# New instruction lists for the last two head pairs of an LSH attention, and a last eviction dealt between ACT and VectorE

## The chip, the cores and the metric

One core of one Trainium2 chip runs the whole program. The metric is the device time of one execution in microseconds, as the median of several runs; lower is better. The program before the change takes 677.83 us (three runs, 676.93 to 678.04).

## What is computed

The reference is an attention in which a query only sees the keys of its own hash bucket, followed by a top-1 mixture of experts (MoE) over the tokens that the attention gives. Inputs are fp32: q, k and v of 4 batches x 8 heads x 768 positions x 64, a projection to 6 hash bits, a gate, and 8 experts of 512 -> 1024 -> 512. Cut to what matters:

```python
q_bits = (einsum('bhsd,dk->bhsk', q, proj) > 0); k_bits = (einsum('bhsd,dk->bhsk', k, proj) > 0)
mask = bucket(q_bits)[..., :, None] == bucket(k_bits)[..., None, :]
scores = where(mask, q @ k.T / sqrt(64), -1e9)
attn = exp(scores - max) / (sum + 1e-9)          # per head, 768 x 768
x = (attn @ v)  ->  3072 tokens x 512
e = argmax(x @ w_gate);  gate = softmax(x @ w_gate)[e]
y = gate * (relu(x @ w1[e]) @ w2[e])
```

## The kernel before

**Work and stages.** The 32 heads are taken as 16 pairs, g = 0 to 15. Each pair has 12 score tiles (128 queries of one head against all 768 keys; two heads x six blocks of queries). The MoE follows: tokens are sorted by expert in DRAM (`sorted_rows`), each expert's rows are read back, and two matrix multiplications per expert follow. Every fp32 operand of the MoE is split into a high and a low part, and three products are summed.

**Step letters.** A pair is written as a list of short names that `step` (L1101 onwards) turns into instructions in that order; a "-" behind a name means the pair before. Pair 0 has the list HEAD, pairs 1 to 13 PLAN, pair 14 NEXT and pair 15 LAST. The scheduler keeps the order of the list on each engine, so a list sets five queues at once. The steps that the prediction speaks of:

- S: scores of one tile, four matmuls on PE (L307, L309) into the PSUM tile "s" (3 buffers). R: masked minimum on VectorE (DVE, L319), which frees that tile. X: exp on ACT (L325).
- T: four transpositions on PE (L339) into the PSUM tile "t" (2 buffers); E: their copy to SBUF, on ACT (L406, suffix a) or DVE (L404, suffix v). Some tiles are turned another way, by step D: a 32x32 block transposition on DVE (L376), and after the last of a pair 16 DMAs (L383) that SyncE (SP) issues, into `pt` (for pair 15 `pq`).
- V: probabilities times values on PE, 24 matmuls. In pairs up to 14, V0 and V2 (L415) are the two halves of the tiles that the 16 DMAs turned, eight DMAs for each half; V1 (L429) takes the tiles turned on PE. In pair 15, V0 takes the tiles of T and V1 the others (both L429). O is the copy of the result (ACT, L445), M the reciprocal of the sums (DVE), K the product with the gate's weights (PE, L470), L its copy to the token rows `xr` (DVE, L480).
- C: one scatter of 128 token rows to `sorted_rows`, an indirect DMA that GpSimd (POOL) issues (L599). Y0: two DMAs on SP that read the first expert's rows into `xd` (L810). x, g, h: these rows transposed on PE (L867) and split (ACT L869, DVE L871).
- W: load of expert weights by SP (`raw`, or `xhe`, a tile that serves as a load buffer first; L765). n and t: the high part of a quarter of a weight chunk (nP on POOL L1034, nA on ACT L1032) and its low part (tP on POOL, tV on DVE, both L1040), taken in turn from a list of 16 quarters.
- m: first matrix multiplication (L888), u and d its relu and low part (ACT L902, DVE L904); the second is L963.

**What holds a step.** Steps on one engine run strictly in order. A scatter (C) that comes behind Y0 in the list writes `sorted_rows`, which Y0's DMAs read, so it waits until both `xd` loads have landed.

**The tail.** The last tile of tokens (98 rows) is done in two halves of 256 columns by `youts` (L984): 24 matmuls each (L1000), a copy scaled by the gate value (first half DVE L1006, second ACT L1004), and an indirect DMA out (L1007). `FIRST` (L947) is the order in which the second matrix multiplication of the first rows sums its eight hidden blocks; each needs its u and d done.

Of the kernel before, what the change touches and what calls it, by code (L numbers as in the profile page):

```python
# [11 lines left out]
AF = mybir.ActivationFunctionType  # L12
OP = mybir.AluOpType
AX = mybir.AxisListType

B, H, S, D = 4, 8, 768, 64
# [5 lines left out]
DM = H * D  # L22
N = B * S
# [8 lines left out]
M0 = float(2 ** 34)  # L32
# [22 lines left out]
def lsh_attention_moe(ctx, tc, qk, qk2, v, proj, wg, w1, w1p, w2, w2p, out):  # L55
    nc = tc.nc
# [80 lines left out]
    C = {}  # L137
# [607 lines left out]
    P2 = {}  # L745
# [43 lines left out]
    XG, IX, XH, HH, YT, GT = {}, {}, {}, {}, {}, {}  # L789
# [107 lines left out]
    M1 = {}  # L897
# [46 lines left out]
            t = len(range(q, nb, 4))  # L944
            nc.sync.dma_start(YR[n][32 * q:32 * q + 32, :t, 128 * a:128 * a + 128], YB[n][32 * a:32 * a + 32, q::4][:, :t])

    FIRST = (6, 1, 5, 3, 2, 4, 0, 7)  # L947

    def yout(n, j, mid=None):
        r, o, c = PH[n]  # L950
# [3 lines left out]
        if n + 1 == len(PH) and j + 1 == len(tiles_of(c)):  # L954
            youts(n, j, i, pw)
            return
        if by_token(n):
            p = ps.tile([128, 512], F32, name="s", bufs=3)
            k = 0
            for f in range(8) if n else FIRST:  # L960
                w = CH[4 * r + 2 + f // 4]
# [24 lines left out]
    def youts(n, j, i, pw):  # L986

        r = PH[n][0]
        y = P2["p"].tile([128, DM], F32, name="y", bufs=2)
        ix = P2["p"].tile([128, 2], I32, name="ix2")  # L990
        for s in range(2):
            nc.vector.tensor_scalar(ix[:, s:s + 1], IX[n][:, j:j + 1], 2.0, float(s), op0=OP.mult, op1=OP.add)
        for s in range(2):
            cs = slice(s * DM // 2, (s + 1) * DM // 2)
            p = ps.tile([128, 512], F32, name="s", bufs=3)
            k = 0
            for f in range(8):
                w = CH[4 * r + 2 + f // 4]
                for a, b in ((0, 0), (1, 0), (0, 1)):
                    nc.tensor.matmul(p[:pw, :DM // 2], HH[n][b][:, f, i:i + pw], w[:, a, f % 4, cs],  # L1000
                                     start=(k == 0), stop=(k == 23))
                    k += 1
            if s:
                nc.scalar.activation(y[:pw, cs], p[:pw, :DM // 2], AF.Copy, scale=GT[n][:pw, j:j + 1])  # L1004
            else:
                nc.vector.tensor_scalar(y[:pw, cs], p[:pw, :DM // 2], GT[n][:pw, j:j + 1], None, op0=OP.mult)  # L1006
            st = nc.gpsimd.indirect_dma_start(out=out.rearrange("n (s d) -> (n s) d", s=2),  # L1007
                                              out_offset=bass.IndirectOffsetOnAxis(ap=ix[:pw, s:s + 1], axis=0),
                                              in_=y[:pw, cs], in_offset=None, bounds_check=2 * N - 1, oob_is_err=False)
            for q in outs:  # L1010
                tc.declare_no_dep(st.ins, q.ins, reason="other parts of the rows")
            outs.append(st)
# [10 lines left out]
    def weight_half(op, x):  # L1023
# [33 lines left out]
    """.split()  # L1057

    NEXT = """
        Z2 S1 S0 P5 R0 G Z2 S8 S3 M0- H R1 R3 T50- Z2 Z2 X0 T51- Q Q R8 S2 T52- S9 R2 E50a- E51a- E52v- Q X1 P1 R9 Z2  # L1060
        D0 A2 X2 V1- X3 S5 S4 S6 V0- V2- O1- R4 R5 I S7 X4 X8 Q X9 D1 X5 S10 T41 W0 W1 S11 P3 P4 T40 W2 P6 R6 B D2 O0-
        P0 X6 W3 R7 R10 T42 A1 K1- E41a E40v X10 K0- P2 U X7 E42v R11 C A0 N L1- P7 L0- C X11 C
    """.split()

    LAST = """
        nP S3 C nA T30- E30a- T50- tP S0 R3 T31- C T51- tP S1 W4 T32- S2 nP E50v- E31a- X3 T52- tP S4 E52a- E51v- S5 R1
        S9 nP R2 E32a- R0 R5 X2 V1- nP S7 X0 X1 D1 X5 Y0 R4 S8 X4 R9 S6 D0 T20 R6 tP O1- R8 V0- nP X9 nP X6 M0- R7 X8
        nA V2- T21 C tV E21v S11 T41 nP E20a O0- R11 tP T22 E41a S10 nP tP E22a T40 K1- tP X11 x2 x0 K0- R10 X10 L1- X7
        E40v g2 L0- tP W5 g0 M0 nP T50 h2 E50a V0 h0 T51 T42 O0 E42a nA K0 T30 E30a tP T31 E51v M1 T52 L0 m1 E31a tP
        E52v r0 r0 r0 u1 T32 m6 r0 E32v W6 V1 u6 m7 O1 r0 K1 nP tV m5 m3 W7 tP r0 u5 d6 d1 nP c0 tP nA u7 L1 r1 r1 r1  # L1070
        r1 m2 u3 m0 m4 tP d5 u2 d7 r1 r1 d3 u4 d2 c1 u0 nP d4 tP d0
    """.split()

    SCAT = {}
# [188 lines left out]
    for n in range(1, len(PH)):  # L1263
        c0 = 4 * (PH[n][0] + 1)
# [28 lines left out]
    with tc.If(C["n"] > 0):  # L1293
        with tc.For_i(0, C["n"], 1) as i:
# [16 lines left out]
            p = ps.tile([128, 512], F32, name="t", bufs=2)  # L1311
# [5 lines left out]
            for f in range(8):  # L1317
                p = ps.tile([128, 512], F32, name="t", bufs=2)
# [3 lines left out]
            p = ps.tile([128, 512], F32, name="s", bufs=3)  # L1322
            for f in range(8):
                nc.tensor.matmul(p, ht[:, f], wb[:, f], start=(f == 0), stop=(f == 7))
            y = sp.tile([128, DM], F32, name="oy")
# [32 lines left out]
```

## Time and profile before

| | |
|---|---|
| median of 3 runs | 677.83 us (676.93, 677.83, 678.04) |
| profiled execution, its own time | 676.77 us |
| its span, first to last instruction | 675.0 us |
| mean granted TensorE clock | 0.999 |
| PE busy | 665.9 us (99%) |
| DVE, ACT, POOL busy | 467.4, 409.7, 468.0 us |
| DMA | 138.51 MB, mean 205 GB/s |

The span leaves 1.8 us of the profiled time outside it. In the rows below, times are microseconds from the span's start; "busy" is time in which an engine computed, and what stands in brackets behind a row is how long the engine had been idle before it and which instruction or DMA ended that idle time.

### The profile page before, as it was taken

How to read it: one execution, taken by the hardware profiler on the slowest of the kernel's cores; microseconds unless marked ns; L12 is line 12 of the kernel's file. 1: busy time of each engine (PE TensorE's matmuls, PEld its weight loads, DVE VectorE, ACT ScalarE, POOL GpSimd, SP SyncE). 2: the span in 40 equal slices, each digit the busy share in tenths (PEclk: the TensorE clock that was granted, in tenths of full speed). 3: DMA queues.
4: the chain of work that ended last, by engine and by line, in shares of the span. 5: the costliest groups of instructions: out<-in, count | busy, mean ns of one | idle time of the engine just before them, and what ended most of it. 6: DMA issues, size and time to landing. Idle time of an engine off the chain costs nothing.

```text
span 675.0 us, 12607 instructions
## 1 busy us (share of the span) xinstructions
PE 665.9 (99%) x4359; PEld 564.6 (84%) x4359; DVE 467.4 (69%) x878; ACT 409.7 (61%) x817; POOL 468.0 (69%) x524
## 2 busy tenths in 40 slices
PE   8999999999999999999999999999999999999997
PEld 4777887788777787788777888899999999989896
DVE  8999889988899889898984545351443645363761
ACT  7977887788778887878775225443444444534410
POOL 7878666977797779777866646855476684959622
PEclk9999999999999999999999999999999999999999
DMA  7689999888889788987896258657548484867203
GB/s 282 209 247 285 260 267 274 217 243 245 230 241 272 188 236 240 265 236 195 239 291 173 101 192 237 162 180 171 156 160 217 131 214 152 220 204 221 102 12 44
DMA packets 74321, 138.51 MB, mean 205 GB/s; under 512 B 16609, under 2 KB 37345, under 8 KB 74256
## 3 DMA queue, kind: packets, MB, share of 16 engines
q1 hardware_dynamic: 66528, 118.57, 61.7%
q0 software_dynamic: 7584, 19.10, 9.7%
q8 instruction: 35, 0.57, 0.4%
q14 instruction: 30, 0.25, 0.2%
q10 hardware_dynamic: 144, 0.02, 0.0%
HBM read 63.39 MB, written 26.33 MB: 133 GB/s over the span
## 4 chain that ended last, share of the span: by engine, by line
PE 95%; ACT 2%; issue 1%; DVE 1%; POOL 0%; POOLq 0%
PE s L888 22%; PE t L415 12%; PE s L927 11%; PE s L307 10%; PE s L963 10%; PE s L309 10%; PE t L339 8%; PE t L429 7%; PE t L470 3%; PE t L264 2%; PE t L104 1%; ACT e L325 1%; ACT qk L215 1%; ACT pq L406 0%; POOL out_dram L1007 0%
## 5 line engine op out<-in xcount | busy, mean ns | idle before, releaser
L325 ACT ACTIVATE e<-e,m 128x768 f32<-128x768 f32 x192 | 178.2, 930 | 37.2 <-DVE e L319 35.6
L319 DVE TENSOR_SCALAR_CACHE_REDUCE e<-s 128x768 f32<-128x768 f32 x192 | 176.1, 951 | 26.2 <-PE s L309 20.3
L784 POOL TENSOR_TENSOR w<-raw,w 128x512 fp32r<-128x512 f32 x112 | 142.3, 1298 | 32.1 <-ACT w L783 31.0
L888 PE MATMUL s<-xh,w 128*128 128x456 f32 (+6 forms) x672 | 123.9, 345 | 0.0
L888 PEld LDWEIGHTS s<-xh,w 128*128 128x128 f32 x672 | 120.0, 188 | 3.1
L904 DVE SCALAR_TENSOR_TENSOR hh<-s,hh 128x256 fp32r<-128x256 f32 (+7 forms) x64 | 35.5, 555 | 89.6 <-ACT hh L902 89.5
L376 DVE STREAM_TRANSPOSE z<-e 128x1536 f32<-128x1536 f32 x52 | 90.7, 1763 | 2.3 <-issue 0.9
L415 PE MATMUL t<-pt,vt 128*64 128x256 f32 x720 | 81.0, 381 | 0.0
L902 ACT ACTIVATE hh<-s 128x256 fp32r<-128x256 f32 (+7 forms) x64 | 31.3, 489 | 75.2 <-PE s L888 75.2
L927 PE MATMUL s<-hh,w 128*128 128x456 f32 (+3 forms) x384 | 74.6, 355 | 0.0
L927 PEld LDWEIGHTS s<-hh,w 128*128 128x128 f32 x384 | 71.3, 188 | 2.7
L415 PEld LDWEIGHTS t<-pt,vt 128*64 128x64 f32 x720 | 50.4, 137 | 27.6 <-issue 3.2
L783 ACT ACTIVATE w<-raw 128x512 fp32r<-128x512 f32 x112 | 66.3, 622 | 9.0 <-DMA raw<-in_w1p_dram 8.7
L339 PE MATMUL t<-ident,e 128*128 128x128 f32 x468 | 68.7, 277 | 1.2 <-DVE pt L404 0.5
L339 PEld LDWEIGHTS t<-ident,e 128*128 128x128 f32 x468 | 53.5, 140 | 18.6 <-ACT pq L406 6.7
L963 PE MATMUL s<-w,hh 128*128 128x512 f32 (+1 forms) x240 | 56.4, 394 | 0.0
L307 PE MATMUL s<-w 80*128 80x384 f32 x192 | 54.2, 363 | 0.0
L406 ACT ACTIVATE pq<-t 128x512 f32<-128x512 f32 x82 | 47.1, 591 | 11.5 <-PE t L339 11.2
L307 PE MATMUL s<-qk 80*128 80x384 f32 x192 | 53.7, 361 | 0.0
L963 PEld LDWEIGHTS s<-w,hh 128*128 128x128 f32 (+1 forms) x240 | 44.7, 187 | 10.6
L309 PE MATMUL s<-qk 128*128 128x384 f32 x192 | 50.0, 341 | 0.0
L309 PE MATMUL s<-w 128*128 128x384 f32 x192 | 49.8, 340 | 0.0
(236 smaller groups left out, 1043.9 us busy)
## 6 DMA issues: line engine op xcount, KB each, us to landing
pt<-z SPq DMA_DIRECT2D x208, 192.0 KB, 4.4
raw<-in_w1p_dram SPq DMA_DIRECT2D x28, 512.0 KB, 3.8
xd<-in_qk_dram SPq DMA_DIRECT2D x14, 768.0 KB, 7.7
sorted_rows<-xr SPq DMA_DIRECT2D x8, 1156.0 KB, 10.9
raw<-in_w_dram SPq DMA_DIRECT2D x18, 512.0 KB, 3.8
raw<-in_w2p_dram SPq DMA_DIRECT2D x16, 512.0 KB, 3.6
vt<-in_v_dram SPq DMA_DIRECT2D x16, 384.0 KB, 5.4
masks<-bits POOLq DMA_DIRECT2D x14, 192.0 KB, 4.7
```

The lines of the kernel that those rows point to most:

```text
L307: nc.tensor.matmul(p[:, a, :HALF], k[0:80, 2, c], k[0:80, 3, n], start=i >= 4, stop=i < 4)
L309: nc.tensor.matmul(p[:, a, :HALF], k[:, 0, c], k[:, 1, n], start=i < 4, stop=i >= 4)
L319: nc.vector.tensor_scalar(e, SC.pop(i)[:, :, :HALF], CEIL, None, op0=OP.min, op1=OP.min, accum_out=m)
L325: nc.scalar.activation(e, e, AF.Exp, bias=m, scale=-1.0, accum_out=SM[g][:, 3 * hf + t, s:s + 1])
L339: nc.tensor.transpose(o[:, j, w], e[w][:, kt // 3, (kt % 3) * 128:(kt % 3) * 128 + 128], ident)
L376: nc.vector.transpose(z[:, :, o].rearrange("p g (k i) -> p g k i", i=32), e)
L415: nc.tensor.matmul(PV[u][s * 64:(s + 1) * 64].rearrange("p (t b a i) -> p a t b i", t=4, b=2, a=2)[:, h], VT[g][:, kt, s, :], PT[u][:, h:: ...
L783: nc.scalar.activation(w[:, 0, a], r, AF.Copy)
L784: nc.gpsimd.tensor_tensor(w[:, 1, a], r, w[:, 0, a], op=OP.subtract)
L888: nc.tensor.matmul(p[:, :c], w[:, a, d, fs], x[:, b, d, :c], start=(k == 0), stop=(k == 11))
L927: nc.tensor.matmul(p[:, :c], w[:, a, f % 4, ms], h[b][:, f, :c], start=(k == 0), stop=(k == 23))
L963: nc.tensor.matmul(p[:pw], HH[n][b][:, f, i:i + pw], w[:, a, f % 4], start=(k == 0), stop=(k == 23))
```

## The change

Three edits. The lists NEXT (pair 14) and LAST (pair 15) are replaced by new ones, which hold nearly the same steps in another order and in places on another engine. `FIRST` gets another order. In `youts` the second half's copy is cut in two: ACT takes 144 columns and DVE the other 112. Core of the diff (one line of each list stands for it):

```diff
-    FIRST = (6, 1, 5, 3, 2, 4, 0, 7)
+    FIRST = (1, 6, 5, 3, 2, 0, 4, 7)
...
             if s:
-                nc.scalar.activation(y[:pw, cs], p[:pw, :DM // 2], AF.Copy, scale=GT[n][:pw, j:j + 1])
+                c1, c2 = slice(DM // 2, DM // 2 + 144), slice(DM // 2 + 144, DM)
+                nc.scalar.activation(y[:pw, c1], p[:pw, :144], AF.Copy, scale=GT[n][:pw, j:j + 1])
+                nc.vector.tensor_scalar(y[:pw, c2], p[:pw, 144:DM // 2], GT[n][:pw, j:j + 1], None, op0=OP.mult)
...
     NEXT = """
-        D0 A2 X2 V1- X3 S5 S4 S6 V0- V2- O1- R4 R5 I S7 X4 X8 Q X9 D1 X5 S10 T41 W0 W1 S11 P3 P4 T40 W2 P6 R6 B D2 O0-
+        P5 S3 Z2 S0 Z2 G R0 S1 T51- Z2 H Q Z2 E51a- S9 R1 R3 X1 T50- S8 T52- S2 R8 R9 V0- E50a- E52a- R2 I X0 Q X8 S5
+        S4 A2 M0- S6 D0 P7 X2 P1 X9 R5 R4 V1- V2- P4 T41 Q Q P0 X3 X4 Z2 W0 W1 S7 S10 D1 T40 X5 A0 O1- A1 O0- D2 R6 B
...
     LAST = """
-        S9 nP R2 E32a- R0 R5 X2 V1- nP S7 X0 X1 D1 X5 Y0 R4 S8 X4 R9 S6 D0 T20 R6 tP O1- R8 V0- nP X9 nP X6 M0- R7 X8
-        nA V2- T21 C tV E21v S11 T41 nP E20a O0- R11 tP T22 E41a S10 nP tP E22a T40 K1- tP X11 x2 x0 K0- R10 X10 L1- X7
+        V1- R1 S9 R0 R2 S8 W4 R5 tP R4 X2 nA D1 Y0 nP S7 C X0 X5 X1 R9 V0- S6 nP R8 D0 X4 X8 R6 nP nA nP O1- T20 X9 R7
+        V2- E20v X6 nP tP T21 E21v S10 tP tP M0- T22 tV S11 tP T41 O0- x2 T40 E22a K1- R11 E41a X7 R10 x0 K0- X11 L1-
```

**Place 1: POOL in pair 15, around the third scatter.** Before (`w_4154` is the weight chunk whose first two quarters and next two are loaded into `xhe`; the row with DMAHW5 and DMAHW4 is the scatter that waits for the `xd` loads):

```order
L1034 CAST w_4154<-xhe 128x512 [waits DMAHW4_49,DMAHW3_49,DMAHW5_49,DMAHW2_49,DMAHW6_49,DMAHW1_49,DMAHW7_49,DMAHW0_49,DVE_49]
L1040 TENSOR_TENSOR w_4039<-raw,w_4039 128x512 [waits Pool_49]
L1034 CAST w_4154<-xhe 128x512
L1034 CAST w_4154<-xhe 128x512 [waits DMAHW1_49]
L598 MEMSET spacer 1x1
L599 DMA sorted_rows<-xr,slot 25600x578 [waits DMAHW5_49,DMAHW4_49]
L1034 CAST w_4271<-raw 128x512 [waits DMAHW3_49,DMASW7_49,PE_49]
```

After, with the same chunk named `w_4166` (the lines of the n and t steps are two higher):

```order
L1036 CAST w_4166<-xhe 128x512 [waits DMAHW4_49,DMAHW3_49,DMAHW5_49,DMAHW2_49,DMAHW6_49,DMAHW1_49,DMAHW7_49,DMAHW0_49,DVE_49]
L598 MEMSET spacer 1x1 [waits Pool_49]
L599 DMA sorted_rows<-xr,slot 25600x578 [waits DMAHW5_49,DMAHW4_49]
L1036 CAST w_4166<-xhe 128x512
L1036 CAST w_4166<-xhe 128x512 [waits DMAHW2_49]
L1036 CAST w_4227<-raw 128x512 [waits DMAHW3_49,DMASW6_49,PE_49]
```

The scatter stood behind all three of POOL's casts of `xhe`; now two of the three stand behind the scatter.

**Place 2: DVE in the same stretch.** Before, from the low part of an `xhe` quarter (tV) to the last copy of pair 14's token rows:

```order
L1040 TENSOR_TENSOR w_4154<-xhe,w_4154 128x512 [waits DMAHW4_49,DMAHW3_49,DMAHW5_49,DMAHW2_49,DMAHW6_49,DMAHW1_49,DMAHW7_49,DMAHW0_49,Pool_49]
L404 COPY pt<-t 128x4x2x64 [waits PE_49]
L319 TENSOR_SCALAR e,m<-s 128x768 [waits PE_49,Activation_49] x2
L480 TENSOR_TENSOR xr<-t,r 128x3x144 [waits DVE_49,PE_49]
L404 COPY pt<-t 128x4x2x64
L480 TENSOR_TENSOR xr<-t,r 128x3x144 [waits PE_49]
```

After:

```order
L1042 TENSOR_TENSOR w_4166<-xhe,w_4166 128x512 [waits DMAHW2_49,Pool_49]
L319 TENSOR_SCALAR e,m<-s 128x768 [waits PE_49,Activation_49]
L319 TENSOR_SCALAR e,m<-s 128x768 [waits Activation_49]
L480 TENSOR_TENSOR xr<-t,r 128x3x144 [waits DVE_49,PE_49]
L404 COPY pt<-t 128x4x2x64
L480 TENSOR_TENSOR xr<-t,r 128x3x144 [waits PE_49]
```

The low part waits on DMAHW2 and POOL now, as the third cast of place 1 waits on DMAHW2: it takes the quarter that POOL casts behind the scatter. The five instructions that follow it are those that stood there before, less one copy ahead of them.

**Place 3: PE in pair 14, the products of pair 13.** Before, L429 (V1) comes first, then three score tiles, then both halves L415 (V0, V2):

```order
L429 MATMUL t<-pq,vt 64x256 x7
...
L309 MATMUL s<-qk 128x384 x2
L415 MATMUL t<-pt,vt 64x8x32 [waits DMAHW4_49,DMAHW5_49,DMAHW3_49,DMAHW6_49,DMAHW2_49,DMAHW7_49,DMAHW1_49,DMAHW0_49]
L415 MATMUL t<-pt,vt 64x8x32 x11
L415 MATMUL t<-pt,vt 64x8x32 [waits DMAHW4_49,DMAHW5_49,DMAHW3_49,DMAHW6_49,DMAHW2_49,DMAHW7_49,DMAHW1_49,DMAHW0_49]
L415 MATMUL t<-pt,vt 64x8x32 x11
```

After, from V0's second row on:

```order
L415 MATMUL t<-pt,vt 64x8x32 x11
L307 MATMUL s<-qk 128x384 [waits DVE_49]
...
L309 MATMUL s<-qk 128x384 x2
L429 MATMUL t<-pq,vt 64x256 [waits Activation_49]
L429 MATMUL t<-pq,vt 64x256 x11
L415 MATMUL t<-pt,vt 64x8x32 [waits DMAHW4_49,DMAHW3_49,DMAHW5_49,DMAHW2_49,DMAHW6_49,DMAHW1_49,DMAHW7_49,DMAHW0_49]
```

V0 stands where V1 stood, ahead of three score tiles, and V1 and V2 follow them. The two copies of the tiles turned on PE (E52 and E40) that stood on DVE in this pair stand on ACT.

On SP, pair 14's 16 DMAs (`pt<-w`) had one `xhe` load in front of them and one behind; now both stand behind them, and so the `xd` loads have one load more between them and the 16. In the tail, the built program lets DVE's new part wait for ACT's: `L1006 TENSOR_SCALAR y<-s,gate 98x112 [waits Activation_49]`.

## Rows read from the trace of the kernel before

**Rows 1.** The page: busy time by engine, and the chain that ended last.
```profile
PE 665.9 (99%) x4359; PEld 564.6 (84%) x4359; DVE 467.4 (69%) x878; ACT 409.7 (61%) x817; POOL 468.0 (69%) x524
...
PE 95%; ACT 2%; issue 1%; DVE 1%; POOL 0%; POOLq 0%
```

**Rows 2.** Busy time by stretch: length, five engines' busy us, PEclk, DMA share, GB/s.
```profile
351.00:362.70 11.70, 11.49 (x96) 9.14 (x96) 7.82 (x18) 7.61 (x15) 5.30 (x8) 1.00 0.82 244
388.00:640.00 252.00, 252.00 (x1323) 235.18 (x1323) 117.83 (x188) 110.79 (x219) 166.85 (x169) 1.00 0.62 182
```

**Rows 3.** The chain in pairs 14 and 15: start us, length us, what.
```profile
320.91 2.93 PE t L429 x24
...
326.14 5.33 PE t L415 x48
...
334.70 0.70 DVE pq L404
...
342.77 0.61 PE s L307 x2
...
362.09 0.62 DVE xr L480
...
362.75 1.53 PE t L429 x24
...
367.79 0.70 DVE pt L404
...
369.58 0.62 DVE xr L480
```

**Rows 4.** DMAs that SP issues, timeline: start us, issuing time us, what, count.
```profile
310.98 11.21 SPq L383 DMA_DIRECT2D pt<-z  x16
...
332.68 13.52 SPq L383 DMA_DIRECT2D pt<-w  x16
346.75 0.38 SPq L765 DMA_DIRECT2D xhe<-in_w_dram  x1
...
348.75 0.88 SPq L810 DMA_DIRECT2D xd<-sorted_rows  x2
```

**Rows 5.** DMA issues of the page: KB each, median us to landing.
```profile
pt<-z SPq DMA_DIRECT2D x208, 192.0 KB, 4.4
```

**Rows 6.** POOL's timeline around the third scatter of pair 15.
```profile
350.61 1.21 POOL L1034 CAST w<-xhe 128x512 fp32r<-128x512 f32 x2
...
357.55 1.01 POOL L599 DMA_INDIRECT sorted_rows<-xr,slot  x1 [5.70 <-DMA pq<-qk]
```

**Rows 7.** DVE's timeline in the same stretch.
```profile
353.87 0.69 DVE L1040 TENSOR_TENSOR w<-xhe,w 128x512 fp32r<-128x512 f32 x1
356.93 0.69 DVE L404 COPY pt<-t 128x512 f32<-128x512 f32 x1 [2.38 <-PE t L339]
358.60 0.96 DVE L319 TENSOR_SCALAR_CACHE_REDUCE e<-s 128x768 f32<-128x768 f32 x1 [0.97 <-PE t L339]
```

**Rows 8.** Groups by shape: busy us, mean ns of one, idle before, releaser.
```profile
L902 ACT ACTIVATE hh<-s 128x354 fp32r<-128x354 f32 x8 | 3.7, 468 | 15.7 <-PE s L888 15.7
...
L902 ACT ACTIVATE hh<-s 128x256 fp32r<-128x256 f32 x8 | 3.1, 382 | 4.2 <-PE s L888 4.2
...
L978 DVE TENSOR_SCALAR y<-s,gate 128x512 f32<-128x512 f32 x9 | 6.7, 745 | 11.0 <-PE s L963 11.0
```

**Rows 9.** The last microseconds, timeline.
```profile
664.34 5.80 PE L1000 MATMUL s<-w,hh 128*98 128x256 f32 x48
...
667.61 0.48 DVE L1006 TENSOR_SCALAR y<-s,gate 98x256 f32<-98x256 f32 x1 [2.20 <-DMA out_dram<-y,ix]
...
670.18 0.47 ACT L1004 ACTIVATE y<-s,gate 98x256 f32<-98x256 f32 x1 [16.36 <-PE s L1000]
```

**Rows 10.** Busy time by stretch behind the last matmul, columns as in rows 2.
```profile
672.00:674.00 2.00, 0.00 (x0) 0.00 (x0) 0.00 (x0) 0.00 (x0) 0.00 (x0) 0.99 0.15 44
674.00:675.00 1.00, 0.00 (x0) 0.00 (x0) 0.00 (x0) 0.00 (x0) 0.00 (x0) 0.50 0.00 0
```

More of the change, by code (lines that the diff above doesn't have):

```diff
@@ L1059, in lsh_attention_moe @@
     NEXT = """
-        Z2 S1 S0 P5 R0 G Z2 S8 S3 M0- H R1 R3 T50- Z2 Z2 X0 T51- Q Q R8 S2 T52- S9 R2 E50a- E51a- E52v- Q X1 P1 R9 Z2
-        D0 A2 X2 V1- X3 S5 S4 S6 V0- V2- O1- R4 R5 I S7 X4 X8 Q X9 D1 X5 S10 T41 W0 W1 S11 P3 P4 T40 W2 P6 R6 B D2 O0-
-        P0 X6 W3 R7 R10 T42 A1 K1- E41a E40v X10 K0- P2 U X7 E42v R11 C A0 N L1- P7 L0- C X11 C
+        P5 S3 Z2 S0 Z2 G R0 S1 T51- Z2 H Q Z2 E51a- S9 R1 R3 X1 T50- S8 T52- S2 R8 R9 V0- E50a- E52a- R2 I X0 Q X8 S5
+        S4 A2 M0- S6 D0 P7 X2 P1 X9 R5 R4 V1- V2- P4 T41 Q Q P0 X3 X4 Z2 W0 W1 S7 S10 D1 T40 X5 A0 O1- A1 O0- D2 R6 B
+        R7 E41a X6 P3 U R10 E40a P6 W2 N X7 T42 S11 X10 W3 E42v P2 K0- R11 C K1- C L0- C L1- X11
     """.split()
     LAST = """
-        nP S3 C nA T30- E30a- T50- tP S0 R3 T31- C T51- tP S1 W4 T32- S2 nP E50v- E31a- X3 T52- tP S4 E52a- E51v- S5 R1
-        S9 nP R2 E32a- R0 R5 X2 V1- nP S7 X0 X1 D1 X5 Y0 R4 S8 X4 R9 S6 D0 T20 R6 tP O1- R8 V0- nP X9 nP X6 M0- R7 X8
-        nA V2- T21 C tV E21v S11 T41 nP E20a O0- R11 tP T22 E41a S10 nP tP E22a T40 K1- tP X11 x2 x0 K0- R10 X10 L1- X7
-        E40v g2 L0- tP W5 g0 M0 nP T50 h2 E50a V0 h0 T51 T42 O0 E42a nA K0 T30 E30a tP T31 E51v M1 T52 L0 m1 E31a tP
-        E52v r0 r0 r0 u1 T32 m6 r0 E32v W6 V1 u6 m7 O1 r0 K1 nP tV m5 m3 W7 tP r0 u5 d6 d1 nP c0 tP nA u7 L1 r1 r1 r1
-        r1 m2 u3 m0 m4 tP d5 u2 d7 r1 r1 d3 u4 d2 c1 u0 nP d4 tP d0
+        nA S3 tP T30- C T50- R3 S0 nP E30a- E50v- T51- C S1 T31- X3 T32- E32a- tP S2 T52- S5 E31a- nA S4 E52a- E51v-
+        V1- R1 S9 R0 R2 S8 W4 R5 tP R4 X2 nA D1 Y0 nP S7 C X0 X5 X1 R9 V0- S6 nP R8 D0 X4 X8 R6 nP nA nP O1- T20 X9 R7
+        V2- E20v X6 nP tP T21 E21v S10 tP tP M0- T22 tV S11 tP T41 O0- x2 T40 E22a K1- R11 E41a X7 R10 x0 K0- X11 L1-
+        X10 E40v g2 W5 L0- tV T50 h2 g0 h0 V0 nA T42 M0 E50a T51 O0 K0 T30 E51v tP W6 E42a T31 nA L0 T52 m1 tV E52v
+        E30a E31a T32 r0 r0 r0 m6 E32a r0 u1 nP V1 r0 O1 nA tP m7 u6 K1 d1 M1 tP u7 m5 r0 u5 m3 d6 W7 nA L1 r1 r1 c0 r1
+        d5 nP tP r1 m2 m4 u3 r1 u4 u2 d7 r1 m0 d3 tP u0 d2 c1 d0 tP d4
     """.split()
```

## The prediction, made before the changed kernel ran

> **What bounds the kernel now.** I read the busy times and the chain that ended last first. PE computes in 665.9 of 675.0 us and holds 95% of the chain [rows 1], so an edit can gain only where PE stands still. Next come the busy times by stretch: from 388 us to 640 us PE is busy in 252.00 of 252.00 us at full granted clock [rows 2], so nothing is to be gained there, and a change in pairs 14 and 15 reaches the end only as an earlier or a later start of that stretch. Third I read the chain in the two pairs. The only pieces that aren't PE's are four of DVE: the copies at 334.70 and 367.79 (0.70 each) and the token rows at 362.09 and 369.58 (0.62 each), 2.64 us in all [rows 3]. That, and score matmuls that are stretched because their PSUM tile comes free late (the first takes 0.61 at 342.77 [rows 3]), is all that better lists could win. Last I read the queues of SP, POOL and DVE in pair 15, since five queues are reordered at once and the question is which of them now stops for what.
>
> **The change, part by part.**
>
> *FIRST.* The order of sums needs the blocks' u and d in that order; the new list deals m, u and d in an order that fits it, and the stretch behind 388 us is full before. Same 24 matmuls per tile: 0.
>
> *Pair 14.* V0 takes V1's place, which was reached at 320.91, where V0 had been reached at 326.14 [rows 3]. V0 needs the first eight of the 16 DMAs that were issued from 310.98 over 11.21 us [rows 4], V2, now behind V1 and about 8 us later, the second eight. The eighth is issued 7/15 into that time, at 316.2, and lands the median 4.4 us [rows 5] later, at 320.6: just in time, so 0 to 0.3 us of waiting. E52 and E40 go from DVE to ACT, so the wait for DVE's copy at 334.70 (0.70 [rows 3]) can go. Net about -0.5 at the end of pair 14. This gain is not in the sum, because the next part sets a time that doesn't depend on it.
>
> *The hold in pair 15.* Here is the step that decides. The third scatter waits for the `xd` loads; before, POOL reached it after 351.8 and stood idle until 357.55 [rows 6]. That cost nothing: the `xhe` casts were done, and DVE's low part (tV) had run at 353.87 [rows 7]. Now two of the casts, the one that tV needs among them, stand behind the scatter. Behind tV on DVE stand two peaks, a token copy, a copy E40 and a token copy; PE's rows of the first expert, its K and pair 15's own V0 wait for them, one after the other.
>
> When does the scatter start? Before, `xd` was issued at 348.75 and the scatter started at 357.55, 8.8 us later [rows 4, 6]; loads ahead of it had to land first. For the new issue I take two ends. The block transpositions of pair 14 end about 1.6 us earlier by their place in the list, so SP's 16 DMAs, at 332.68 before [rows 4], and what follows may go 1.6 earlier; one more `xhe` issue (0.38 [rows 4]) stands between: 348.75 - 1.6 + 0.4 = 347.5. If the 16 DMAs also gain by the load that no longer stands in front of them, 512 KB at the 244 GB/s of this stretch [rows 2] or 2.1 us, it is 345.4. I take the middle, 346.5. That same load now stands ahead of `xd`: 0 to 2.1 us more to land. I take 2.1, since DMA traffic is the limit in this stretch (share 0.82 [rows 2]). Scatter: 346.5 + 8.8 + 2.1 = 357.4, ends 345.4 + 8.8 = 354.2 and 347.5 + 10.9 = 358.4.
>
> From the scatter to V0: scatter 1.01, two casts 1.21 [rows 6], tV 0.69 [rows 7], and then what took 4.15 us before, from the first peak at 358.60 [rows 7] to V0 at 362.75 [rows 3], for the same five DVE instructions with PE's between. Sum 7.06: V0 at 357.4 + 7.06 = 364.5, against 362.75, **+1.7 us** (ends -0.4, where PE itself is the limit as in rival A, and +2.7).
>
> *Behind V0.* Two of the four DVE pieces lie here, at 367.79 and 369.58 [rows 3]. The new list gives one copy here to ACT and leaves the other on DVE. I take one of the two as gone, **-0.6** (ends -1.3 and 0). The MoE's weights are split at most two microseconds later than before, by POOL, which is ahead of PE there: 0.
>
> *The tail.* The last copy took ACT 0.47 for 256 columns [rows 9]. ACT's 0.468 and 0.382 us for 354 and 256 columns [rows 8] give 0.88 ns a column: 144 columns take 0.37. DVE's 0.745 for 512 [rows 8] and 0.48 for 256 [rows 9] give 1.0 ns a column: 112 take 0.33. Side by side the pair would end after 0.37, 0.10 earlier; one after the other, with 0.04 between them as for other hand-overs of the chain, after 0.74, 0.27 later. No row shows two engines on one PSUM tile at once; the built order has DVE's part wait for ACT's, so I take **+0.3**. The Trainium skill, "PSUM — Partial Sum Buffer", section "PSUM bank collisions raise a hardware error", speaks against this edit too: two engines may not touch the same bank and quadrant of partitions at once, even at different columns, and a dependency is put between them. By that rule the term is +0.27, and without it -0.10; no run here shows it yet.
>
> **Sum.** +1.7 - 0.6 + 0.3 = +1.4 us. Against the profiled execution's own 676.77 that is 678.2; it lies 1.06 below the median 677.83, so against the median I forecast **679.3 us**. About 0.2% (1.36 us: below 676.47 or above 679.19) is what a measurement can tell from no change, so the forecast lies on that edge.
>
> **The rivals.**
>
> *A. No hold: the `xd` loads land early.* Unheld, DVE would reach tV at about 357.0, behind a copy that started at 356.93 before [rows 7]. The hold bites only if scatter and casts (2.22) end after that, so if the scatter starts after 354.8. For it: my early end is 354.2. Against: it needs both favours, the early issue and the free load. PE then sets V0 at about 362.4: -0.35 - 0.6 + 0.3 = -0.65, 677.2 us.
>
> *B, the other side. DVE is off the chain.* With two copies fewer on DVE in pair 14, V0 moved and no hold, all four DVE pieces (2.64) go, with, as an estimate, half of the stretched 0.61 at 342.77 [rows 3]: -2.9 + 0.3 = -2.6, 675.2 us. It decides from the same point, a scatter by 354.8, and if ACT, busy 7.61 of 11.70 us there [rows 2], takes the copies without being late itself. Against: the list leaves tV ahead of the peaks.
>
> *C. Pair 14's V0 waits for all 16 DMAs.* If the first half needs more than the first eight, V0 waits for a DMA issued at 322.2 that lands at 326.6 [rows 4, 5]: 5.7 us behind 320.9. Some 2.1 us of it fit into the hold's wait, so +3.6 on the forecast, 682.9. Against: the built order gives each half its own wait.
>
> *D. The clock falls in the hold.* PE would stand still for some 2 to 3 us in pieces. For it: the granted clock did fall to 0.50 at the very end. Against: after the last matmul, which ended at 670.14 [rows 9], it was still 0.99 from 672 to 674 [rows 10], longer than any piece of the hold. A fall would double some 2 us of matmul: 681.3. The Trainium skill, "TensorE: Matmul & The Clock Gate", section "What's actually happening", has the clock follow how busy PE has been; the two rows agree.
>
> **How the numbers follow.** Forecast 0.54, A 0.20, B 0.15, C 0.05, D 0.06. The predicted time is the forecast's, 679.3. Its own range is 678.0 to 681.0, from the ends of the hold (+0.9 late, about -1.3 with an early issue), so about half of it lies above 679.19: 0.28 slower, 0.26 same. A is same but for its early edge (0.17 same, 0.03 faster), B faster, C and D slower. Together faster 0.18, same 0.43, slower 0.39. The range that leaves out no more than 2 in 10 reaches down through A and half of B and up to the late end: 675.4 to 681.2.
>
> **What would show it.** Right: in the changed profile POOL's third scatter starts near 357 with two casts of `xhe` behind it; DVE's tV waits for POOL and starts after 359; pair 15's V0 starts after 364; the tail shows ACT 0.37 and DVE 0.33 one after the other. Wrong: a scatter before 355, tV without idle time ahead of it, V0 of pair 15 before 362.5, or two tail copies that overlap. V0 of pair 14 much after 321.2 would be C; a PEclk under 1.00 around 360, D.

## The result, and the profile after

The changed kernel takes 687.64 us (median of 16 executions) against 677.85 us (16 executions of the kernel before); the ratio, which leaves out three slow executions (689.25, 689.48 and 1692.72), is 1.0116 with a 95% interval of 1.0092 to 1.0140; the two medians alone give 1.0144. So it is slower, by far more than forecast, and outside the range. Its executions don't agree with each other as those of before do (676.85 to 679.61): they reach from 678.97 to 689.48, and one took 1692.72, which nothing here explains.

The profiled execution took 687.23 us with a span of 685.4, 10.4 more than before. The busy times and the chain that ended last, of the changed kernel, answer to [rows 1]:

```profile
PE 667.7 (97%) x4359; PEld 565.7 (83%) x4359; DVE 479.8 (70%) x878; ACT 413.7 (60%) x823; POOL 465.2 (68%) x519
...
PE 86%; issue 4%; POOL 3%; ACT 3%; DMA 2%; DVE 2%; POOLq 0%; SPq 0%; DVEq 0%; ACTq 0%
```

PE's work grew by 1.8 us only, but DVE's busy time grew by 12.4 us although it has the same number of instructions; 7.05 of it is one instruction in pair 15 (3.9 more are the copies L978 of the last stage, which scale rows by their gate values; POOL's scatters wait for them, PE doesn't). POOL's timeline there, the counterpart of [rows 6]:

```profile
351.04 0.61 POOL L1036 CAST w<-xhe 128x512 fp32r<-128x512 f32 x1 [4.61 <-DMA xhe<-in_w_dram]
351.59 0.09 POOL L598 MEMSET spacer<- 1x1 f32 x1
358.10 1.00 POOL L599 DMA_INDIRECT sorted_rows<-xr,slot  x1 [6.42 <-DMA pq<-qk]
359.12 1.17 POOL L1036 CAST w<-xhe 128x512 fp32r<-128x512 f32 x2
360.23 1.17 POOL L1036 CAST w<-raw 128x512 fp32r<-128x512 f32 x2
361.37 1.25 POOL L1042 TENSOR_TENSOR w<-raw,w 128x512 fp32r<-128x512 f32 x1
362.60 3.69 POOL L1042 TENSOR_TENSOR w<-xhe,w 128x512 fp32r<-128x512 f32 x3
366.25 1.25 POOL L1042 TENSOR_TENSOR w<-raw,w 128x512 fp32r<-128x512 f32 x1
```

The bracket behind the scatter names the DMAs into `pq`, but the chain that ended last puts the wait down to the `xd` loads. A piece of the chain, and SP's timeline:

```profile
349.45 7.86 DMA xd<-sorted_rows
```

```profile
331.31 12.80 SPq L383 DMA_DIRECT2D pt<-w  x16
...
348.90 0.90 SPq L810 DMA_DIRECT2D xd<-sorted_rows  x2
```

DVE's timeline, the counterpart of [rows 7]:

```profile
360.32 7.74 DVE L1042 TENSOR_TENSOR w<-xhe,w 128x512 fp32r<-128x512 f32 x1 [1.58 <-POOL w L1036]
367.98 0.94 DVE L319 TENSOR_SCALAR_CACHE_REDUCE e<-s 128x768 f32<-128x768 f32 x1
```

Quarters of the weights are counted from 0, in the order in which the list takes them; tV is the low part of quarter 6. The hold that was forecast is there: the scatter starts at 358.10 with two `xhe` casts behind it, and tV waits 1.58 us for POOL and starts at 360.32. But tV then takes 7.74 us, where the same instruction took 0.69 [rows 7]. It ends at 368.06, 0.56 us after POOL's run of nine instructions without a pause, from 359.12 to 367.50. PE stood still meanwhile (its timeline):

```profile
368.99 1.12 PE L867 MATMUL s<-ident,xd 128*128 128x128 f32 x4 [7.34 <-DVE e L319]
```

and the granted clock fell to 0.50, its lower level (1.2 of 2.4 GHz). Busy times by stretch (length, then PE, PEld, DVE, ACT, POOL, PEclk, DMA share, GB/s):

```profile
366.00:369.00 3.00, 0.01 (x1) 0.01 (x1) 3.00 (x4) 0.03 (x1) 1.51 (x2) 0.50 0.01 3
369.00:371.00 2.00, 1.72 (x6) 1.32 (x7) 1.93 (x4) 2.00 (x5) 0.00 (x0) 0.50 0.00 0
371.00:373.00 2.00, 2.00 (x11) 1.74 (x12) 0.77 (x2) 1.42 (x4) 0.00 (x0) 0.57 0.00 0
373.00:375.00 2.00, 2.00 (x32) 1.78 (x34) 1.89 (x5) 0.58 (x1) 0.00 (x0) 1.00 0.26 32
```

In the chain, pair 15's V0 starts at 372.95, against 362.75 before [rows 3], and its V1 at 384.55, against 374.71:

```profile
372.95 4.09 PE t L429 x48
...
384.55 4.09 PE t L429 x24
```

So +10.2 at V0 and +9.8 at V1. Behind that, 0.3 us go at the rows of the second part (L850), where PE waits 0.6 us for DVE's L856 instead of 0.3, and the rest in the tail, which did what was forecast: ACT's 144 columns and DVE's 112 run one after the other.

```profile
680.36 0.38 ACT L1005 ACTIVATE y<-s,gate 98x144 f32<-98x144 f32 x1 [16.36 <-PE s L1000]
680.77 0.33 DVE L1006 TENSOR_SCALAR y<-s,gate 98x112 f32<-98x112 f32 x1 [2.73 <-ACTq L1295]
```

From the last matmul's end (680.32) to the last scatter's issue it is 1.09 us (681.41), before 0.82 (670.14 to 670.96): +0.27.

### The profile page after: what moved, and what is told of

Same layout as the page of the kernel before. It is cut to its first block, busy times and chain, and to the rows that moved or that the text cites. A ratio compares the mean times of both kernels' runs of the same rounds, so it can differ in the third digit from the quotient of the medians.

```text
span 685.4 us, 12614 instructions
## 1 busy us (share of the span) xinstructions
PE 667.7 (97%) x4359; PEld 565.7 (83%) x4359; DVE 479.8 (70%) x878; ACT 413.7 (60%) x823; POOL 465.2 (68%) x519
## 4 chain that ended last, share of the span: by engine, by line
PE 86%; issue 4%; POOL 3%; ACT 3%; DMA 2%; DVE 2%; POOLq 0%; SPq 0%; DVEq 0%; ACTq 0%
PE s L888 21%; PE s L927 11%; PE t L415 10%; PE s L963 10%; PE s L307 8%; PE s L309 8%; PE t L429 6%; PE t L339 6%; PE t L470 3%; PE t L264 2%; DMA xd<-sorted_rows 1%; ACT e L325 1%; DMA sorted_rows<-xr,slot 1%; ACT qk L215 1%; POOL sorted_rows L599 1%
## 5 line engine op out<-in xcount | busy, mean ns | idle before, releaser
L376 DVE STREAM_TRANSPOSE z<-e 128x1536 f32<-128x1536 f32 x52 | 90.7, 1763 | 2.3 <-DMA pt<-z 1.2
L415 PE MATMUL t<-pt,vt 128*64 128x256 f32 x720 | 81.4, 381 | 0.2 <-DMA pt<-z 0.2
L415 PEld LDWEIGHTS t<-pt,vt 128*64 128x64 f32 x720 | 50.6, 137 | 27.7 <-issue 3.5
```

Of the source, the lines that this page charges most:

```text
L376: nc.vector.transpose(z[:, :, o].rearrange("p g (k i) -> p g k i", i=32), e)
L415: nc.tensor.matmul(PV[u][s * 64:(s + 1) * 64].rearrange("p (t b a i) -> p a t b i", t=4, b=2, a=2)[:, h], VT[g][:, kt, s, :], PT[u][:, h:: ...
```

## The experiments

Two questions: why does one DVE instruction take 7.74 us, and is that all of the loss? Theory P says that a DVE instruction which reads two operands from SBUF can't start while POOL computes one instruction after the other. The Trainium skill, "SBUF — State Buffer", section "Who interferes with whom", has such a rule: a DVE instruction with two SBUF inputs contends with a GpSimd instruction that reads SBUF, and whichever comes second waits for the whole of the other. In the traces here such a wait would stand as busy time of DVE, as in the 7.74 us. Rival Q: the data of that weight quarter, or the DMAs that write `pq` at the time, make this one instruction slow. The first four runs stand beside a median of 676.97 us for the kernel before, the others beside 677.83 to 677.93.

**Its work given to POOL.**

```diff
-   ... M0- T22 tV S11 tP T41
+   ... M0- T22 tP S11 tP T41
```

> The changed kernel with one step on another engine: the low part of weight quarter 6, the DVE instruction that took 7.74 us, is done by POOL at the same place of the list. Theory P (a DVE instruction that reads two SBUF operands does not start while POOL computes one instruction after the other): the peaks start near 358.7 instead of 367.98, pair 15's V0 near 362.5; but the next such DVE instruction, the low part of quarter 8, meets the same run of POOL near 362 and lasts until that run ends near 368.7, so it takes 4 us or more, and some of the loss stays: 678 to 682 us. Rival Q (quarter 6's data or the DMAs that write pq make the one instruction slow): quarter 8's low part takes 0.69, the loss goes: 676 to 677.5 us.

682.32 us, ratio 1.0088 (1.0056 to 1.0120), 0.3 above P's range. The 7.74 us are gone, and the next such instruction, quarter 8's, has them instead. DVE's timeline:

```profile
366.52 4.80 DVE L1042 TENSOR_TENSOR w<-raw,w 128x512 fp32r<-128x512 f32 x1
```

POOL's timeline:

```profile
364.60 4.94 POOL L1042 TENSOR_TENSOR w<-xhe,w 128x512 fp32r<-128x512 f32 x4
369.51 1.26 POOL L1042 TENSOR_TENSOR w<-raw,w 128x512 fp32r<-128x512 f32 x1
```

POOL's run ends at 370.77, DVE's instruction at 371.32, again 0.55 later. Against Q: another quarter, from another buffer, does the same. (The expected times lie some 4 us early: V0 starts at 366.66. In this execution the loads landed later than in the changed kernel's profile, POOL's first cast of `xhe` started at 353.79 instead of 351.04, and PE had stood 2.19 us for O1, behind ACT's cast of quarter 7. The run on the scatter behind the casts shows that stop again.)

**The same wait, with one operand.** `J` is a row sum on DVE over the cast of quarter 6.

```diff
-   ... M0- T22 tV S11 tP T41
+   ... M0- T22 J tP S11 tP T41
+            nc.vector.tensor_reduce(f, CH[c][:, 0, a].bitcast(F32), axis=AX.X, op=OP.add)
```

> As the first run, but DVE keeps, in the place of the low part of quarter 6, an instruction that waits for the same POOL cast and reads one SBUF operand of the same size (a sum over the row, used by nobody); the low part itself is POOL's. So the hold behind the scatter stays as in the changed kernel, and only the second SBUF operand is gone. Theory P: that instruction takes about 0.6 us from 360.3 on, V0 of pair 15 starts near 365, the clock stays at 1.00: 679 to 683 us, 1.5 to 2.5 more than the first run unless quarter 8's wait hides it. Rival Q: it takes several us as before, about 687 us.

680.90 us, ratio 1.0053 (1.0036 to 1.0069). DVE's timeline:

```profile
361.34 0.69 DVE L1212 TENSOR_REDUCE one<-w 128x1 f32<-128x512 f32 x1 [0.97 <-POOL w L1036]
...
365.91 4.42 DVE L1042 TENSOR_TENSOR w<-raw,w 128x512 fp32r<-128x512 f32 x1
```

POOL's timeline:

```profile
361.24 1.17 POOL L1036 CAST w<-raw 128x512 fp32r<-128x512 f32 x2
...
363.61 4.94 POOL L1042 TENSOR_TENSOR w<-xhe,w 128x512 fp32r<-128x512 f32 x4
368.52 1.26 POOL L1042 TENSOR_TENSOR w<-raw,w 128x512 fp32r<-128x512 f32 x1
```

With one operand, behind the same wait and beside POOL's casts, it takes 0.69 us; in the same execution the next instruction with two takes 4.42, to 0.55 us after POOL's run. For the low parts P holds, and Q falls.

What the run shows, it shows of a row sum. That every DVE instruction with one SBUF operand is free of POOL doesn't follow, and the traces speak against it: in the last stage of the changed kernel, L978 scales rows of one SBUF tile, each by one gate value, and takes 0.43 us at the least; beside a scatter's issue and two of POOL's low parts it takes 3.57, to 0.31 us after them. DVE's timeline, then POOL's, changed kernel:

```profile
543.50 3.57 DVE L978 TENSOR_SCALAR yr<-yr,gate 128x512 f32<-128x512 f32 x1
```

```profile
544.22 2.54 POOL L784 TENSOR_TENSOR w<-raw,w 128x512 fp32r<-128x512 f32 x2
```

The block transpositions (L376), also with one SBUF operand, take 1.72 to 1.78 us in all 57 cases, most of them beside POOL's work. So the number of operands alone doesn't tell which instructions are held.

This run also measures the forecast's hold alone: from the scatter (359.12) to V0 (366.05) it is 6.9 us, where the forecast had 7.06.

**Gaps in POOL's run.** `J` is here a write of one element by POOL.

```diff
-   ... R6 nP nA nP O1- T20 X9 R7 V2- E20v X6 nP tP T21 E21v S10 tP tP M0- T22 tV S11 tP T41
+   ... R6 nP nA J nP J O1- T20 X9 R7 V2- E20v X6 nP J tP J T21 E21v S10 tP J tP J M0- T22 tV S11 tP J T41
```

> The changed kernel with a one-element POOL write put between the nine POOL instructions that follow quarter 6's cast (about 0.1 us each); DVE's two low parts stay. Theory P, in the form that any POOL instruction that reads no SBUF lets DVE in: quarter 6's low part takes at most one POOL instruction plus 0.69, so under 2 us, and the run comes to 679 to 681 us. Theory P, in the form that POOL must be idle for DVE to get in: still about 7.7 us or more, 687 to 689 us. Rival Q: no difference, 687 to 688 us.

689.15 us, ratio 1.0136 (1.0076 to 1.0196): no help, though one of the four executions took 681.51. DVE's timeline:

```profile
360.72 7.93 DVE L1042 TENSOR_TENSOR w<-xhe,w 128x512 fp32r<-128x512 f32 x1 [0.97 <-POOL spacer L1210]
```

POOL's timeline, the first gap and the end of the run:

```profile
360.61 0.09 POOL L1210 MEMSET spacer<- 1x1 f32 x1
...
366.85 1.25 POOL L1042 TENSOR_TENSOR w<-raw,w 128x512 fp32r<-128x512 f32 x1
```

Six such gaps go by while the instruction waits, and it ends at 368.65, 0.55 after POOL's last. So here POOL instructions that read no SBUF didn't let DVE in.

**The same in the kernel before.**

```diff
-   ... T21 C tV E21v S11 ... K0- R10 X10 L1-
+   ... T21 C E21v S11 ... K0- R10 tV X10 L1-
```

> The kernel before with one edit: DVE's low part of an xhe quarter is moved from 353.87, where POOL stands idle, behind the second peak, to about 361.3, where POOL computes without a pause until 365.4. Nothing else of the change is in it, and there is no hold. Theory P: the instruction lasts from 361.3 to about 366, so over 4 us, V0 of pair 15 starts near 367, 4 us later: 681 to 684 us. Rival Q: it takes 0.69, and at most 0.7 us is lost: 677.9 to 678.6 us.

678.26 us, ratio 1.0045 (1.0011 to 1.0080). The median lies below P's range and inside Q's, but the instruction took 1.84 us, neither Q's 0.69 nor P's over 4. The nine executions are of two kinds: six between 677.54 and 678.55 and three between 683.30 and 685.27. The profiled one is of the first kind. DVE's timeline:

```profile
360.41 1.84 DVE L1040 TENSOR_TENSOR w<-xhe,w 128x512 fp32r<-128x512 f32 x1
```

POOL's timeline:

```profile
360.40 1.26 POOL L1040 TENSOR_TENSOR w<-xhe,w 128x512 fp32r<-128x512 f32 x1
361.62 1.10 POOL L1034 CAST w<-raw 128x512 fp32r<-128x512 f32 x1
...
365.13 1.26 POOL L1040 TENSOR_TENSOR w<-raw,w 128x512 fp32r<-128x512 f32 x1
```

Here DVE came in behind the first POOL instruction and ended at 362.25; POOL's cast behind it took 1.10, where 0.62 is usual, so POOL waited in its turn. So the wait can end at the first boundary between two POOL instructions. The three long executions lie 5 to 7 us above the others; a wait to 0.55 us after POOL's run, which ends at 366.39, would make the instruction 4.7 us longer. None of the three was profiled, so that this is what they are isn't shown. The length of the wait differs from case to case, and the changed kernel's spread of 678.97 to 689.48 would fit that.

**The scatter behind the casts.** Is the order at the scatter the main loss after all?

```diff
-   ... D1 Y0 nP S7 C X0 ... R6 nP nA nP O1- T20
+   ... D1 Y0 nP S7 X0 ... R6 nP C nA nP O1- T20
```

> The changed kernel with the third scatter moved behind POOL's casts of quarters 5 and 6, as in the kernel before. Then DVE's low part of quarter 6 has its cast early and comes to run at about 358.7, while POOL still waits for the xd loads or issues the scatter and computes nothing. Theory P: it takes 0.69, peaks start near 359.5 and pair 15's V0 near 363; but quarter 8's low part meets POOL's run near 364 and lasts until the run ends near 368: 678 to 682 us, mostly faster than the first run of the study. If instead the hold behind the scatter were the main loss, all of it goes: 677 us.

680.86 us, ratio 1.0057 (1.0028 to 1.0085), within P's range. So 6.8 us go with that order and the wait that it brings, and 3.0 stay. In the profiled execution quarter 6's low part took 0.94 and quarter 8's 1.66. A stop that I hadn't listed shows: ACT's cast of quarter 7 comes late, with O1 behind it, and PE stands for O1. The old list had that cast behind O1. In the changed kernel's own profile the stop isn't there; in five of the seven further profiles with that order it is, for 0.69 to 3.35 us. Those five are the ones in which POOL's first cast of `xhe` starts late too, at 352.43 us or after; where it starts by 351.09, PE doesn't stand. ACT's timeline:

```profile
355.73 0.63 ACT L1034 ACTIVATE w<-xhe 128x512 fp32r<-128x512 f32 x1 [4.41 <-issue]
```

PE's timeline:

```profile
356.69 0.66 PE L339 MATMUL t<-ident,e 128*128 128x128 f32 x4 [3.35 <-ACT ot L445]
```

**Both low parts on POOL.** No DVE low part is left beside POOL's run; the scatter stays ahead of the casts.

```diff
-   ... M0- T22 tV S11 ... L0- tV T50 h2
+   ... M0- T22 tP S11 ... L0- tP T50 h2
```

> The changed kernel with the low parts of quarters 6 and 8 both on POOL, so that DVE has no instruction with two SBUF operands while POOL computes; the scatter stays ahead of the casts, NEXT and the tail stay as changed. Theory P: no long DVE instruction, no bimodal times, all runs within 1 per cent: 676.5 to 679 us. POOL's run gets 1.25 us longer per step, which nobody waits for unless the weights of the first matrix multiplication come late. Rival R (the new order is slow by itself, the long instruction only shows it): over 680 us.

681.94 us, ratio 1.0047 (1.0029 to 1.0065): P's 676.5 to 679 missed, R's range met. One of six executions took 690.64; it wasn't profiled, and since neither quarter's low part is DVE's here, not all of the spread is explained by their wait. No DVE instruction of the stretch is long any more, V0 starts at 363.95, but V1 only at 378.75, 4.0 later than before. POOL's timeline:

```profile
362.91 4.96 POOL L1042 TENSOR_TENSOR w<-xhe,w 128x512 fp32r<-128x512 f32 x4
```

ACT's timeline:

```profile
367.90 1.08 ACT L869 ACTIVATE xhe<-s 128x512 fp32r<-128x512 f32 x2 [4.67 <-POOL w L1042]
```

So there is a second hold. The split of the first expert's rows (L869) writes `xhe`, the tile that served as load buffer, and waits until POOL has read the last quarter from it. POOL does that late because its whole run stands behind the scatter. Behind L869 on ACT stand copies of T, and PE waits for them.

**Three parts mended.** The scatter behind the casts, quarter 8's low part on POOL, the tail as before.

```diff
+   ... R6 nP C nA nP O1- T20 ... L0- tP T50 h2
-                nc.vector.tensor_scalar(y[:pw, c2], p[:pw, 144:DM // 2], GT[n][:pw, j:j + 1], None, op0=OP.mult)
```

> The changed kernel with three edits undone or mended: the scatter behind the casts, quarter 8's low part on POOL, the last eviction by ACT alone. Theory P: quarter 6's low part takes 0.69 while POOL waits, no DVE instruction over 2 us in the stretch, the tail 0.27 us shorter than the changed kernel's: 675.5 to 678 us, at or slightly under the kernel before. Rival R: over 680 us.

679.93 us, ratio 1.0042 (1.0017 to 1.0067); ten of the twelve executions lie between 679.12 and 681.50, and two took 688.51 and 689.32. Quarter 6's low part took 0.95 in the profiled one, but the median lies above P's 678: PE stood 1.69 us for O1 again, and DVE 2.23 us for ACT's L869, the second hold, which the next but one run tests.

**The new list of pair 14 alone.**

```diff
-    NEXT = """ Z2 S1 S0 P5 R0 G ...
+    NEXT = """ P5 S3 Z2 S0 Z2 G R0 ...
```

> The kernel before with the new list of pair 14 alone; pair 15, FIRST and the tail are as before. No DVE low part is moved into POOL's run. Pair 14 ends 0.5 us earlier as in the changed kernel's trace (336.57 for 337.18). Both theories: 677 us or up to 1 us less, unless the xhe loads behind the 16 DMAs let the casts come later, which then would cost 0 to 2 us in pair 15.

677.76 us, ratio 1.0001 (0.9990 to 1.0012): no change. So the loss comes with LAST, `FIRST` and the tail; `FIRST` wasn't run by itself, but in the changed kernel's profile all but 0.6 us has arisen before the second matrix multiplication, where it acts.

**The scatter behind all work on xhe.** This tests the second hold.

```diff
-   ... D1 Y0 nP S7 C X0 ... R6 nP nA nP O1- ... X6 nP tP T21 ... M0- T22 tV S11 tP T41 ... L0- tV T50
+   ... D1 Y0 nP S7 X0 ... R6 nP nA O1- ... X6 tP T21 ... M0- T22 tP S11 tP C nP nP T41 ... L0- tP T50
```

> As the run with both low parts on POOL, with one more move: the third scatter (which waits for the xd loads) stands behind all of POOL's work on the xhe quarters, and the casts of quarters 8 and 9 behind it. The theory in addition to P, from that run's trace (ACT's split of the first expert's rows, L869, at 367.90 after 4.67 us of waiting for POOL's low parts of the same xhe buffer): the scatter holds POOL, POOL holds that buffer, and ACT stands still with the copies that PE waits for queued behind. Then L869 should start near 362 here, pair 15's V0 near 362.5, its V1 near 374.5 instead of 378.75, and the time be 676.5 to 678.5 us. If the new order is slow for another reason, over 680 us.

679.27 us, ratio 1.0024 (1.0014 to 1.0034); the twelve executions lie between 677.88 and 680.57, with none apart from the others. The median is 0.8 above the expected range, V0 (363.62) and V1 (375.19) are 1.1 and 0.7 late; the mechanism is as expected. POOL's timeline:

```profile
353.63 4.98 POOL L1042 TENSOR_TENSOR w<-xhe,w 128x512 fp32r<-128x512 f32 x4
```

ACT's timeline:

```profile
362.81 1.06 ACT L869 ACTIVATE xhe<-s 128x512 fp32r<-128x512 f32 x2
```

L869 starts without idle time ahead of it, 5.1 us earlier than in the run with both low parts on POOL, and V1 3.6 us earlier.

**And two more mends.** Quarter 7's cast behind O1, and the old tail.

```diff
-   ... R6 nP nA O1- T20
+   ... R6 nP O1- nA T20
```

> As the run before it, with quarter 7's cast on ACT moved behind the copy O1 that PE waits for, and the last eviction by ACT alone again. In the traces so far that cast waited for its load with O1 queued behind it (PE stood 1.69 and 3.35 us for O1 in two of the runs). Theory: 0.3 to 1.5 us less than the run before it, 675.8 to 677.5 us, at or slightly under the kernel before. If the cast on ACT is not what held O1: the same as the run before it less 0.3.

679.26 us, ratio 1.0016 (1.0007 to 1.0026). The expected 675.8 to 677.5 is missed by 1.8 us. The two intervals overlap, so a gain over the run before it isn't shown; PE hadn't stood for O1 in that run's profile, so there was little to win. No version here beats the kernel before.

**What the steps add up to**, by medians against 677.83 to 677.93: the new lists and the tail with neither hold, +1.4 (679.27); POOL held by the scatter ahead of its `xhe` work, +2.7 more (681.94); DVE's low parts beside POOL's run, +5.7 more (687.64). The middle and last step overlap in time, so the split between them holds for this order of taking them away only. Of the first +1.4 a part is placed: the profiled execution of that run is 1.1 us longer than that of before, 0.5 of it by the start of the second matrix multiplication (388.96 for 388.47) and 0.6 behind it, 0.27 in the tail and 0.3 at L850. What the rest is stays open.

## Why the prediction was wrong

- **What bounds.** Right: of the 10.4 us in the profiled execution all but 0.6 arose in pair 15.
- **Pair 14.** Right. V0 waited 0.24 us for its DMAs, forecast 0 to 0.3, and pair 15's first score started at 336.57 instead of 337.18, forecast 0.5 earlier. PE's timeline of the changed kernel:

```profile
321.34 2.81 PE L415 MATMUL t<-pt,vt 128*64 128x256 f32 x24 [0.24 <-DMA pt<-z]
```

  So rival C fell. As forecast, the gain was swallowed by the next step; by itself it is too small to be measured.
- **The hold.** The place and the mechanism were right, and the start came out near the forecast: scatter 358.10 (forecast 357.4, ends 354.2 to 358.4), tV at 360.32 (forecast 359.6). That was luck in part, as two errors cancel. SP issued `xd` at 348.90, later than the forecast's 346.5 and than its late end of 347.5: the 16 DMAs did start 1.37 us earlier, but from the end of their issue to `xd`, with both `xhe` loads between, it took SP 4.79 us instead of 2.55. And the scatter followed 9.2 us after the issue, not 10.9.
- **The step that failed: "tV 0.69".** It was taken from the one row in which POOL stood idle [rows 6, 7], and moved into a place where POOL had nine instructions queued, because the scatter held POOL and tV back together. It measured 7.74: +7.05 of the 8.45 us by which V0 missed the forecast (372.95 for 364.5). The rest is the scatter's 0.7 and 0.8 behind the stop, at the lower clock: from the first peak to V0 it is 4.97 (367.98 to 372.95) where it was 4.15. (The three overlap by 0.1.)
- **Rows of before that would have told it.** The group of all low parts of transposed rows on DVE, which read two SBUF tiles, has twice the mean of its ordinary duration; the view by line gives 518, 580 and 3556 ns as least, median and longest of the 28. Groups of DVE, and two timelines (DVE, then POOL), kernel before:

```profile
L841 DVE TENSOR_TENSOR xh<-xt,xh 128x456 fp32r<-128x456 f32 (+6 forms) x28 | 32.0, 1181 | 1.9 <-ACT xh L839 1.1
```

```profile
489.58 3.67 DVE L841 TENSOR_TENSOR xh<-xt,xh 128x408 fp32r<-128x408 f32 x2
```

```profile
489.76 2.55 POOL L784 TENSOR_TENSOR w<-raw,w 128x512 fp32r<-128x512 f32 x2
```

  The two DVE instructions take 3.67 us where the median would give 1.2, and they end after POOL's two. The shapes of the group don't explain it: they go from 354 to 456 columns. A reader who asks why a group's mean is twice its median is led to POOL's row beside it. I read only the row of the one instruction that moved.
- **Behind V0, -0.6.** 384.55 - 372.95 is 11.60 against 11.96: -0.36, within the ends. The part behind 388 us, put at nothing, lost the 0.3 at L850.
- **"By POOL, which is ahead of PE there: 0".** Wrong too. It asked whether the weights come in time, and not who waits for the buffer that POOL reads them from. In the changed kernel the long DVE instruction covers this wait; with that away it costs 2.7 us (681.94 against 679.27). ACT's queue wasn't in the sum either: quarter 7's cast ahead of O1 cost nothing in this profile, but up to 3.35 us in others.
- **The tail, +0.27.** Measured 0.27: the two parts don't overlap. The Trainium skill, "PSUM — Partial Sum Buffer", section "PSUM bank collisions raise a hardware error", puts a dependency between two engines on one bank and quadrant, and the trace agrees. As the built program has DVE's part wait for ACT's, no run shows what would happen without that wait.
- **Rivals.** A and B fell with the scatter at 358.10. D came true, but as a consequence: its counter-argument, that no piece of the hold is long enough, rested on 0.69. Its price was forecast at 2 us and came to some 0.8.
- **A slip in the sum.** 677.83 + 1.4 is 679.2, not 679.3; nothing hangs on it.

## What to carry to other kernels

A duration is only good for the neighbours that it was measured beside: before a DVE instruction that reads two SBUF operands, or scales an SBUF tile, is moved, see what POOL does at its new place, and look at the longest of its kind in the trace, not at the mean. On an engine that works in order, an instruction that waits for a DMA belongs behind all work that another engine, or the next user of a buffer, waits for. And a gain of half a microsecond ahead of such a hold is worth nothing.

## What was not expected of the hardware

- A DVE instruction with two SBUF operands can wait through several POOL instructions: seven in the changed kernel, and as many, with six gaps of one-element writes between them, in the run with gaps. The Trainium skill, "SBUF — State Buffer", section "Who interferes with whom", speaks of waiting for the whole of one instruction. Here the wait went on over the boundaries between them. In other cases it ended at the first boundary (1.84 us in the run on the kernel before). What decides this is open, and with it the size of the loss from one execution to the next.
- With one operand in SBUF some DVE instructions aren't held and others are: the row sum took 0.69 beside POOL's casts, the scaled copy L978 3.57 instead of 0.43 beside POOL's low parts.
- The granted clock stood at 0.50, the lower level, from 366 to 371 us. PE had been idle for 7.34 us until 368.99. From 373 us on, with PE busy again, the clock was at 1.00.
